# Background attention placed by a small planner into FFN steps, with a second accumulator bank, grouped k features and loads in halves

## The chip, the cores and the metric

The kernel runs on one core of one Trainium2 chip. The metric is the time of one execution in microseconds (us), the lower the better. The kernel before has a slow state, in which the granted TensorE clock is lower and the run about 5 us longer (fast runs 266.2 to 267.3 us, those with a recorded clock at 0.951 to 0.964; slow runs 270 to 274 at 0.927 to 0.950). Only fast runs are used for times. The trace of the kernel before that is read below fell in the slow state (271.9 us, span 269.8), so some 5 us of what it shows are that state's and not the kernel's.

PE is TensorE's matmul, PEld its weight load, DVE is VectorE, ACT is ScalarE, POOL is GpSimd, SP is SyncE.

## The reference

```python
# q, k, v: (4 batches, 4 heads, 1088, 32); S1, S2: (8, 32); w_in (128, 2048), w_out (2048, 128); all float32
phi(x) = outer(S1 x, S2 x)                     # 64 features for each token and head
kv = phi(k)^T v ;  z = sum(phi(k))             # over the 1088 tokens
attn = (phi(q) kv) / (phi(q) z + 1e-6)
x = attn, heads side by side: (4352, 128)
out = max(x @ w_in, 0)^2 @ w_out
```

For each batch the attention must be finished chunk by chunk (three chunks of 384, 384 and 320 tokens) before the FFN of that chunk can start. So the kernel computes the attention of batch n in the background of the FFN of batch n - 1.

## The kernel before

One FFN step handles one of 16 slices of 128 hidden units for one chunk: `pg` (float16 matmul into PSUM), relu on ACT into `gt`, square on DVE or ACT into `g2`, `po` (float32, two matmul instructions, x2 in the timelines) accumulated over 16 steps. There are 4 x 3 x 16 = 192 steps; `pg` and relu run three steps ahead of `po` (LA = 3). In the traces an instruction of PE or DVE that has to wait also holds up what stands behind it on its engine (below, an `nd` matmul of PE waits 1.65 us, and the FFN's matmuls with it).

The names in code and traces: `kT` is k transposed, `kf` its two feature factors (S1 k and S2 k), `fs` their copy by ACT (the matmuls here all write into tiles of the PSUM pools `psf` and `psa`, called banks below), `kp` their product phi(k), and `kv` the matmuls that sum phi(k)^T v in PSUM. `qT`, `qc`, `qb`, `qa` and `qp` are the same for q. `nd` holds numerator and denominator of attn. The x chain divides them in ten DVE operations, from `den` to `xs` and `beta` (`xs` is scaled for float16; `beta` undoes that at the output). `xp` transposes `xs` on PE, and its copy `xT` is the input of the FFN. `oT`, `op` and `ob` bring the FFN's result to the output.

```python
    # pools: pg 3 banks, po 2, and one bank each for acc, feat, tr
    psf = ctx.enter_context(tc.tile_pool(name="psf", bufs=3, space=bass.MemoryType.PSUM))
    psa = ctx.enter_context(tc.tile_pool(name="psa", bufs=1, space=bass.MemoryType.PSUM))
...
    def a_kp(b, g):
        kf = st[b, "kf", g]
        fs = wpool.tile([128, 3 * 96], F32, tag="fs", name="fs")
        kp = wpool.tile([128, 3 * 256], F32, tag="kp", name="kp", bufs=3)
        segs = [(0, 3, 128)] if g < 2 else [(0, 2, 128), (2, 1, 64)]
        for i, n, w in segs:
            nc.scalar.copy(fs[0:w, 96 * i : 96 * i + 96 * n], kf[0:w, 96 * i : 96 * i + 96 * n])
        for i in range(3):
            w = TW[3 * g + i]
            nc.vector.tensor_tensor(
                out=_ap(kp, 0, w, 256 * i, [[32, 8], [8, 4], [1, 8]]),
                in0=_ap(fs, 0, w, 96 * i, [[4, 8], [1, 4], [0, 8]]),
                in1=_ap(fs, 0, w, 96 * i + 32, [[8, 8], [0, 4], [1, 8]]),
                op=mult,
            )
        st[b, "kp", g] = kp

    def a_kv(b, t):
        if t == 0:
            st[b, "kvp"] = psa.tile([128, 512], F32, tag="acc", name="kvp")
        kvp = st[b, "kvp"]
        kp = st[b, "kp", t // 3]
        w = TW[t]
        for e in range(E):
            nc.tensor.matmul(
                kvp[:, 132 * e : 132 * e + 132],
                kp[0:w, 256 * (t % 3) + 128 * e : 256 * (t % 3) + 128 * e + 128],
                va[b % 2][0:w, 132 * t : 132 * t + 132],
                start=(t == 0 and e == 0),
                stop=(t == NT - 1),
                skip_group_check=True,
            )
...
    def a_nd(b, t):
        ch, o = t // 3, t % 3
        if o == 0:
            st[b, "nd", ch] = psa.tile([128, 512], F32, tag="acc", name="nd")
        nd = st[b, "nd", ch]
        w = TW[t]
        for e in range(E):
            nc.tensor.matmul(
                nd[0:w, 132 * o : 132 * o + 132],
                st[b, "qp", ch, e][:, 128 * o : 128 * o + w],
                st[b, "kvz"][:, 132 * e : 132 * e + 132],
                start=(e == 0),
                stop=(e == E - 1),
            )

    def a_xs(b, ch):

        if ch == 0:
            st[b, "xT"] = bpool.tile([128, S], F16, tag="xT", name="xT")
            st[b, "beta"] = bpool.tile([128, NT], F32, tag="beta", name="beta")
        nd, beta = st[b, "nd", ch], st[b, "beta"]
        xs = wpool.tile([128, 3 * 128], F16, tag="xs", name="xs")
        for o, n, w in ([(0, 3, 128)] if ch < 2 else [(0, 2, 128), (2, 1, 64)]):
            ...  # ten dependent DVE ops: den, rden, mx, m1, mm, mp, rm, sc, xs, beta
...
    def ffn1(i):
        b, ch, c = steps[i]
        n = min(384, S - 384 * ch)
        pg = psf.tile([128, 512], F32, tag="pg", name="pg")
        nc.tensor.matmul(
            pg[:, 0:n],
            w_in[:, 128 * c : 128 * c + 128],
            st[b, "xT"][:, 384 * ch : 384 * ch + n],
        )
        gt = fpool.tile([128, 384], F32, tag="gt", bufs=3, name="gt")
        g2 = fpool.tile([128, 384], F32, tag="g2", name="g2")
        nc.scalar.activation(gt[:, 0:n], pg[:, 0:n], Relu)
        if c % 4 == 3:
            nc.scalar.activation(g2[:, 0:n], gt[:, 0:n], Square)
        else:
            nc.vector.tensor_tensor(out=g2[:, 0:n], in0=gt[:, 0:n], in1=gt[:, 0:n], op=mult)
        g2s[i] = g2

    def ffn2(i):
        b, ch, c = steps[i]
        n = min(384, S - 384 * ch)
        if c == 0:
            st["po", b, ch] = psf.tile([128, 512], F32, tag="po", bufs=2, name="po")
        nc.tensor.matmul(
            st["po", b, ch][:, 0:n],
            w_o[:, 128 * c : 128 * c + 128],
            g2s.pop(i)[:, 0:n],
            start=(c == 0),
            stop=(c == NFF - 1),
        )
...
            # background of batch n, placed by hand in the 48 FFN steps of batch n - 1
            at(4, a_v, n)
            for part in range(3):
                at(5 + part, a_kT, n, part)
            for g in range(3):
                at(8 + 3 * g, a_kf, n, g, psa, "feat")
                at(9 + 3 * g, a_kp, n, g)
            for t in range(NT):
                at(18 + t, a_kv, n, t)
            at(17, a_qT, n, 0)
            at(18, a_qT, n, 1)
            for ch in range(3):
                at(19 + 4 * ch, a_qc, n, ch, psa, "feat")
                at(20 + 4 * ch, a_qb, n, ch)
                at(21 + 4 * ch, a_qa, n, ch, 0)
                at(22 + 4 * ch, a_qa, n, ch, 1)
            at(27, a_kvz, n)
            for ch in range(3):
                for i in range(3):
                    at(29 + 5 * ch + i, a_nd, n, 3 * ch + i)
                at(32 + 5 * ch, a_xs, n, ch)
                at(35 + 5 * ch, a_xp, n, ch)
```

Of the kernel before, what the change touches and what calls it, by code (L numbers as in the profile page):

```python
# [20 lines left out]

@with_exitstack
def kernel(
# [16 lines left out]

    G = S // 32
    DFF = 2048
    NFF = DFF // 128
    NT = (S + 127) // 128
    TW = [min(128, S - 128 * t) for t in range(NT)]
    CHUNKS = [(0, 3), (3, 6), (6, 9)]
    E = 2
    LA = 3

# [12 lines left out]
    psf = ctx.enter_context(tc.tile_pool(name="psf", bufs=3, space=bass.MemoryType.PSUM))  # L62
# [4 lines left out]
    s_nat = cpool.tile([128, 32], F32)  # L67
    nc.gpsimd.memset(s_nat[:], 0.0)
    for h in range(H):
        nc.sync.dma_start(s_nat[32 * h : 32 * h + 8, :], S1[:, :])  # L70
        nc.scalar.dma_start(s_nat[32 * h + 8 : 32 * h + 16, :], S2[:, :])

    def load_qk(dst, src, b, c0, c1, eng):
        eng.dma_start(
            dst[:, c0:c1],
            bass.AP(src.tensor, src.offset + b * H * S * D + c0, [[G * D, 128], [1, c1 - c0]]),
        )

    def load_v(vn, b, eng):

        base = v.offset + b * H * S * D
        for p0 in range(4):
            eng.dma_start(
                _ap(vn, 32 * p0, 32, 0, [[256, H], [1, 256]]),
                bass.AP(v.tensor, base + 8 * p0 * D, [[G * D, 32], [S * D, H], [1, 8 * D]]),
            )
        for p0 in range(2):
            eng.dma_start(
                _ap(vn, 32 * p0, 32, 1024, [[32, H], [1, 32]]),
                bass.AP(v.tensor, base + (32 + p0) * D, [[G * D, 32], [S * D, H], [1, D]]),  # L90
            )
# [7 lines left out]

    alloc_loads(0)  # L100
    load_qk(kn[0], k, 0, 0, 512, nc.sync)
    load_qk(kn[0], k, 0, 512, S, nc.scalar)
    load_v(vn[0], 0, nc.sync)
    load_qk(qn[0], q, 0, 0, 512, nc.scalar)
    load_qk(qn[0], q, 0, 512, S, nc.scalar)

# [3 lines left out]
    for c in range(2):  # L110
        nc.sync.dma_start(
            w_in32[:, 1024 * c : 1024 * c + 1024], moe_w_in[:, 1024 * c : 1024 * c + 1024]
        )
    for c in range(2):
        nc.sync.dma_start(
            _ap(w_o, 0, 128, 1024 * c, [[128, 8], [1, 128]]),
            bass.AP(
                moe_w_out.tensor,
                moe_w_out.offset + c * 1024 * 128,
                [[128, 128], [128 * 128, 8], [1, 128]],  # L120
            ),
        )
# [5 lines left out]
    nc.gpsimd.memset(sq[:], 0.0)  # L128
    iden = cpool.tile([128, 128], F32)
# [3 lines left out]
    hmask = cpool.tile([128, E * 132], F32)  # L133
    nc.gpsimd.memset(hmask[:], 0.0)
    for h in range(H):
        nc.gpsimd.memset(_ap(hmask, 32 * h, 32, 33 * h, [[132, E], [1, 33]]), 1.0)
    va = []
    for i in range(2):
        t_ = cpool.tile([128, NT * 132], F32, tag=f"va{i}", name=f"va{i}")
        nc.gpsimd.memset(_ap(t_, 0, 128, 32, [[33, NT * H]]), 1.0)  # L140
        va.append(t_)
# [22 lines left out]
    def a_v(b):  # L164
        a = va[b % 2]
        nc.gpsimd.tensor_copy(  # L166
            _ap(a, 0, 128, 0, [[33, H], [132, 8], [1, 32]]),
            _ap(vn[b], 0, 128, 0, [[256, H], [32, 8], [1, 32]]),
        )
        nc.gpsimd.tensor_copy(  # L170
            _ap(a, 0, 64, 8 * 132, [[33, H], [1, 32]]),
            _ap(vn[b], 0, 64, 1024, [[32, H], [1, 32]]),
        )

    def a_kT(b, part):
        if part == 0:
            st[b, "kT"] = bpool.tile([128, S], F32, tag="kT", bufs=1, name="kT")
        kT = st[b, "kT"]
        if part < 2:
            nc.vector.transpose(  # L180
                _ap(kT, 0, 128, 64 * part, [[32, 2], [128, 8], [1, 32]]),
                _ap(kn[b], 0, 128, 512 * part, [[256, 2], [32, 8], [1, 32]]),
# [4 lines left out]
    def a_qT(b, part):  # L187
        if part == 0:
            st[b, "qT"] = bpool.tile([128, S], F32, tag="qT", bufs=1, name="qT")
        c0, c1 = ((0, 512), (512, S))[part]  # L190
        nc.vector.transpose(st[b, "qT"][:, c0:c1], qn[b][:, c0:c1])  # L191

    def a_kf(b, g, pool, tag):
        kT = st[b, "kT"]
        kf = pool.tile([128, 512], F32, tag=tag, name="kf")
        for i in range(3):
            w = TW[3 * g + i]
            nc.tensor.matmul(  # L198
                kf[0:w, 96 * i : 96 * i + 96],
                kT[:, 128 * (3 * g + i) : 128 * (3 * g + i) + w],  # L200
                sk[:, :],
            )
        st[b, "kf", g] = kf

    def a_kp(b, g):
        kf = st[b, "kf", g]
        fs = wpool.tile([128, 3 * 96], F32, tag="fs", name="fs")
        kp = wpool.tile([128, 3 * 256], F32, tag="kp", name="kp", bufs=3)
        segs = [(0, 3, 128)] if g < 2 else [(0, 2, 128), (2, 1, 64)]
        for i, n, w in segs:  # L210
            nc.scalar.copy(fs[0:w, 96 * i : 96 * i + 96 * n], kf[0:w, 96 * i : 96 * i + 96 * n])  # L211
        for i in range(3):
            w = TW[3 * g + i]
            nc.vector.tensor_tensor(  # L214
                out=_ap(kp, 0, w, 256 * i, [[32, 8], [8, 4], [1, 8]]),
                in0=_ap(fs, 0, w, 96 * i, [[4, 8], [1, 4], [0, 8]]),
                in1=_ap(fs, 0, w, 96 * i + 32, [[8, 8], [0, 4], [1, 8]]),
                op=mult,
            )
        st[b, "kp", g] = kp  # L220

    def a_kv(b, t):
        if t == 0:
            st[b, "kvp"] = psa.tile([128, 512], F32, tag="acc", name="kvp")
        kvp = st[b, "kvp"]
        kp = st[b, "kp", t // 3]
        w = TW[t]
        for e in range(E):
            nc.tensor.matmul(  # L229
                kvp[:, 132 * e : 132 * e + 132],  # L230
                kp[0:w, 256 * (t % 3) + 128 * e : 256 * (t % 3) + 128 * e + 128],
                va[b % 2][0:w, 132 * t : 132 * t + 132],
# [12 lines left out]
    def a_qc(b, ch, pool, tag):  # L245
        c0 = 384 * ch
        n = min(384, S - c0)
        qc = pool.tile([128, 512], F32, tag=tag, name="qc")
        nc.tensor.matmul(qc[:, 0:n], sq[:, :], st[b, "qT"][:, c0 : c0 + n])  # L249
        st[b, "qc", ch] = qc  # L250

    def a_qb(b, ch):
        n = min(384, S - 384 * ch)
        qb = wpool.tile([128, 384], F32, tag="qb", name="qb")
        nc.vector.stream_shuffle(in_=st[b, "qc", ch][:, 0:n], out=qb[:, 0:n], mask=mask_b)
        st[b, "qb", ch] = qb

    def a_qa(b, ch, e):
        n = min(384, S - 384 * ch)
        qa = wpool.tile([128, 384], F32, tag="qa", name="qa")  # L260
        qp = bpool.tile([128, 384], F32, tag="qp", bufs=4, name="qp")
        nc.vector.stream_shuffle(in_=st[b, "qc", ch][:, 0:n], out=qa[:, 0:n], mask=mask_a[e])  # L262
        nc.vector.tensor_tensor(  # L263
            out=qp[:, 0:n], in0=qa[:, 0:n], in1=st[b, "qb", ch][:, 0:n], op=mult
# [3 lines left out]
    def a_nd(b, t):  # L268
        ch, o = t // 3, t % 3
        if o == 0:  # L270
            st[b, "nd", ch] = psa.tile([128, 512], F32, tag="acc", name="nd")
        nd = st[b, "nd", ch]
        w = TW[t]
        for e in range(E):
            nc.tensor.matmul(  # L275
                nd[0:w, 132 * o : 132 * o + 132],
                st[b, "qp", ch, e][:, 128 * o : 128 * o + w],
# [5 lines left out]
    def a_xs(b, ch):  # L283

        if ch == 0:
            st[b, "xT"] = bpool.tile([128, S], F16, tag="xT", name="xT")
            st[b, "beta"] = bpool.tile([128, NT], F32, tag="beta", name="beta")
        nd, beta = st[b, "nd", ch], st[b, "beta"]
        xs = wpool.tile([128, 3 * 128], F16, tag="xs", name="xs")
        for o, n, w in ([(0, 3, 128)] if ch < 2 else [(0, 2, 128), (2, 1, 64)]):  # L290
            def small(tag, m=4):
                return wpool.tile([128, 12], F32, tag=tag, name=tag)[0:w, 0 : m * n]
            den, rden, mx, m1, sc = (small(x) for x in ("den", "rden", "mx", "m1", "sc"))
            mm, mp, rm = (small(x, 1) for x in ("mm", "mp", "rm"))
            nc.vector.tensor_scalar(
                out=den, in0=_ap(nd, 0, w, 132 * o + 32, [[33, 4 * n]]),
                scalar1=1e-6, scalar2=None, op0=add,
            )
            nc.vector.reciprocal(rden, den)  # L299
            nc.vector.tensor_reduce(  # L300
                out=mx, in_=_ap(nd, 0, w, 132 * o, [[33, 4 * n], [1, 32]]),
                axis=AX, op=amax, apply_absolute_value=True,
            )
            nc.vector.tensor_tensor(out=m1, in0=mx, in1=rden, op=mult)
            nc.vector.tensor_reduce(
                out=mm, in_=_ap(m1, 0, w, 0, [[4, n], [1, 4]]),
                axis=AX, op=amax, apply_absolute_value=True,
            )
            nc.vector.tensor_scalar(  # L309
                out=mp, in0=mm, scalar1=1.0 / 1024.0, scalar2=1.0 / 1024.0, op0=mult, op1=add,  # L310
            )
            nc.vector.reciprocal(rm, mp)
            nc.vector.tensor_tensor(
                out=_ap(sc, 0, w, 0, [[4, n], [1, 4]]),
                in0=_ap(rden, 0, w, 0, [[4, n], [1, 4]]),
                in1=_ap(rm, 0, w, 0, [[1, n], [0, 4]]),
                op=mult,
            )
            nc.vector.tensor_tensor(  # L319
# [226 lines left out]
```

## Time and profile before

| | before |
|---|---|
| time, fast runs of the first measurement | 266.75 us median (266.44 to 267.25) |
| profiled run | 271.9 us, span 269.8, state slow |
| first `pg` matmul | 27.4 us |
| FFN part, first `pg` to last `po` | 27.4 to 263.2 us |

From the page of the kernel before: busy time of the engines and, in 40 equal slices of the span, the busy tenths of PE and the granted clock of TensorE.

```profile
PE 227.8 (84%) x1032; PEld 148.8 (55%) x1032; DVE 162.2 (60%) x469; ACT 137.0 (51%) x319; POOL 8.9 (3%) x29
...
PE   0884996959997779999997697999997779999991
...
PEclk9999597999997997999997979999999997999998
```

PE is the busiest engine, but three times its row sinks to 7 and 6, in the third chunk of each of the first three batches (it also sinks to 6 and 5 in the first batch, between 40 and 61 us). The view of stretches, cut at the ends of FFN chunks, has for each stretch its length, the busy time of each engine with the number of instructions, and the granted clock:

```profile
core 0: us, PE busy (x) PEld busy (x) DVE busy (x) ACT busy (x) POOL busy (x), PEclk, DMA share, GB/s
...
27.40:54.40 27.00, 24.14 (x100) 15.47 (x100) 18.67 (x57) 12.12 (x27) 0.00 (x0) 0.84 0.00 1
54.40:78.20 23.80, 21.03 (x106) 14.28 (x105) 16.88 (x50) 11.56 (x27) 0.00 (x0) 1.00 0.03 9
...
139.80:166.20 26.40, 20.06 (x90) 12.88 (x89) 15.92 (x58) 11.18 (x27) 1.28 (x2) 0.87 0.29 72
...
181.80:202.10 20.30, 20.30 (x104) 14.18 (x103) 14.55 (x37) 10.93 (x27) 0.00 (x0) 1.00 0.04 10
...
239.30:252.50 13.20, 13.20 (x53) 7.52 (x53) 6.57 (x13) 10.38 (x25) 0.00 (x0) 1.00 0.06 16
```

The stretch 181.8 to 202.1 is full: PE has no gap, so with its clock at 1.00 only less PE work could shorten it. The stretch 139.8 to 166.2 has 6.3 us without PE work, and its clock is 0.87. No stretch has DVE or ACT busy for its whole length (the largest share is 79%, ACT from 239.3 to 252.5): no other engine is full. The view of waits, for PE alone (who waited, for whom, us in total, how often, longest):

```profile
PE nd L275 <- DVE beta L325: 9.1, 5, 2.5
PE kf L198 <- DVE kT L185: 7.9, 1, 7.9
PE xp L336 <- DVE xs L319: 6.0, 6, 1.5
...
PE kf L198 <- DVE kT L180: 2.7, 1, 2.7
```

The second line is the start of the kernel; the others are stalls inside the FFN part. One of them in the timeline (start, duration, engine, line, operation; in brackets the idle time before and what ended it):

```profile
80.70 0.16 DVE L295 TENSOR_SCALAR den<-nd 128x12 f32<-128x12 f32 x1
...
82.60 0.56 DVE L319 TENSOR_TENSOR xs<-nd,sc 128x384 f16<-128x384 f32 x1
83.07 0.15 DVE L325 TENSOR_TENSOR beta<-mp 128x3 f32<-128x3 f32 x1
...
83.30 0.69 PE L275 MATMUL nd<-kvz,qp 128*128 128x132 f32 x4 [1.65 <-DVE beta L325]
...
83.96 1.27 PE L371 MATMUL po<-g_729,w_o 128*128 128x320 f32 x2
...
88.11 0.70 PE L371 MATMUL po<-g_776,w_o 128*128 128x320 f32 x2
```

The x chain runs for 2.5 us from `den` to `beta`. PE reaches the next chunk's `nd`, which needs the same accumulator bank, 1.65 us too early and stands still, with all FFN work behind it. Then the pair of `po` matmuls takes 1.27 us; in the same view an undisturbed pair takes 0.70. This stall is paid twice, once as idle time and once as a slow clock: the packed trace's clock records, which the views show only as means, have half clock for 3.41 us from 83.95.

### The profile page before, as it was taken

How to read it: one execution, taken by the hardware profiler on the slowest of the kernel's cores; microseconds unless marked ns; L12 is line 12 of the kernel's file. 1: busy time of each engine (PE TensorE's matmuls, PEld its weight loads, DVE VectorE, ACT ScalarE, POOL GpSimd, SP SyncE). 2: the span in 40 equal slices, each digit the busy share in tenths (PEclk: the TensorE clock that was granted, in tenths of full speed). 3: DMA queues.
4: the chain of work that ended last, by engine and by line, in shares of the span. 5: the costliest groups of instructions: out<-in, count | busy, mean ns of one | idle time of the engine just before them, and what ended most of it. 6: DMA issues, size and time to landing. Idle time of an engine off the chain costs nothing.

```text
span 269.8 us, 3312 instructions
## 1 busy us (share of the span) xinstructions
PE 227.8 (84%) x1032; PEld 148.8 (55%) x1032; DVE 162.2 (60%) x469; ACT 137.0 (51%) x319; POOL 8.9 (3%) x29
## 2 busy tenths in 40 slices
PE   0884996959997779999997697999997779999991
PEld 0682464737665545567665464567764535555660
DVE  2654774686765673767766636576768563545440
ACT  1220552464363446765463355767445446787861
POOL 4201000000000200000000100000000000000000
PEclk9999597999997997999997979999999997999998
DMA  5992000000006400001004600001001000001000
GB/s 141 276 324 68 0 2 0 0 7 26 0 0 166 115 0 4 20 1 32 0 0 139 139 2 0 26 1 32 0 0 29 2 1 0 24 1 29 7 24 24
DMA packets 11897, 11.23 MB, mean 42 GB/s; under 512 B 1896, under 2 KB 10344, under 8 KB 11880
## 3 DMA queue, kind: packets, MB, share of 16 engines
q1 hardware_dynamic: 11384, 10.17, 14.0%
q10 hardware_dynamic: 496, 0.86, 1.2%
q8 instruction: 8, 0.13, 0.2%
q14 instruction: 9, 0.07, 0.1%
HBM read 8.79 MB, written 2.23 MB: 41 GB/s over the span
## 4 chain that ended last, share of the span: by engine, by line
PE 72%; DVE 19%; ACT 3%; issue 2%; DMA 2%; ACTq 1%; POOL 0%; DVEq 0%; POOLq 0%
PE po L371 38%; PE pg L352 10%; PE nd L275 7%; PE kvp L229 7%; PE kf L198 4%; PE qc L249 3%; DVE xs L319 3%; DVE mx L300 2%; DMA kn<-in_k_dram 2%; ACT gt L359 2%; DVE qp L263 1%; DVE mp L309 1%; DVE rden L299 1%; PE op L391 1%; PE xp L336 1%
## 5 line engine op out<-in xcount | busy, mean ns | idle before, releaser
L359 ACT ACTIVATE gt<-pg 128x384 f32<-128x384 f32 (+1 forms) x192 | 89.2, 471 | 85.6 <-PE pg L352 79.9
L352 PE MATMUL pg<-xT,w_in 128*128 128x384 f16 (+1 forms) x192 | 63.5, 333 | 0.6 <-ACT xT L342 0.6
L275 PE MATMUL nd<-kvz,qp 128*128 128x132 f32 (+1 forms) x144 | 25.1, 302 | 11.9 <-DVE beta L325 9.1
L275 PEld LDWEIGHTS nd<-kvz,qp 128*128 128x128 f32 (+1 forms) x144 | 21.5, 198 | 21.9 <-issue 16.3
L352 PEld LDWEIGHTS <-w_in 128*128 128x128 f16 x192 | 19.8, 103 | 16.3 <-issue 3.4
L198 PE MATMUL kf<-sk,kT 128*128 128x96 f32 (+1 forms) x72 | 12.6, 324 | 10.6 <-DVE kT L185 7.9
L214 DVE TENSOR_TENSOR kp<-fs 128x256 f32<-128x256 f32 (+1 forms) x36 | 13.9, 443 | 8.6 <-ACT fs L211 8.6
L198 PEld LDWEIGHTS kf<-sk,kT 128*128 128x128 f32 (+1 forms) x72 | 11.3, 227 | 14.1 <-issue 8.0
L342 ACT COPY xT<-xp 128x384 f16<-128x384 f16 (+1 forms) x12 | 5.5, 456 | 22.3 <-PE xp L336 22.3
L263 DVE TENSOR_TENSOR qp<-qa,qb 128x384 f32<-128x384 f32 (+1 forms) x24 | 12.9, 537 | 6.3 <-PE nd L275 5.3
L229 PEld LDWEIGHTS kvp<-va_124,kp 128*128 128x128 f32 (+1 forms) x72 | 10.7, 190 | 5.3 <-issue 1.1
L262 DVE STREAM_SHUFFLE qa<-qc 128x384 f32<-128x384 f32 (+1 forms) x24 | 13.5, 562 | 0.0
L249 PE MATMUL qc<-qT,sq 128*128 128x384 f32 (+1 forms) x24 | 10.6, 526 | 3.3 <-DVE qT L191 3.3
L397 ACT ACTIVATE ob<-op,beta 128x128 f32<-128x128 f32 (+1 forms) x36 | 10.5, 363 | 4.6 <-PE op L391 4.5
L229 PEld LDWEIGHTS kvp<-va_122,kp 128*128 128x128 f32 (+1 forms) x72 | 10.7, 211 | 3.5 <-POOL va_122 L166 0.7
L229 PE MATMUL kvp<-va_124,kp 128*128 128x132 f32 (+1 forms) x72 | 11.2, 279 | 0.0
L336 PE MATMUL xp<-iden_114,xs 128*128 128x128 f16 (+1 forms) x36 | 5.3, 249 | 7.0 <-DVE xs L319 6.0
L229 PE MATMUL kvp<-va_122,kp 128*128 128x132 f32 (+1 forms) x72 | 11.1, 299 | 0.0
L336 PEld LDWEIGHTS <-xs 128*128 128x128 f16 (+1 forms) x36 | 3.5, 113 | 12.8 <-DVE xs L319 8.1
L211 ACT COPY fs<-kf 128x288 f32<-128x288 f32 (+2 forms) x16 | 4.9, 335 | 6.3 <-PE kf L198 6.3
L319 DVE TENSOR_TENSOR xs<-nd,sc 128x384 f16<-128x384 f32 (+2 forms) x16 | 7.3, 455 | 0.5
L382 ACT COPY oT<-po 128x384 f32<-128x384 f32 (+1 forms) x12 | 5.5, 460 | 3.2 <-PE po L371 2.2
(649 smaller groups left out, 407.2 us busy)
## 6 DMA issues: line engine op xcount, KB each, us to landing
vn<-in_v_dram SPq DMA_DIRECT2D x16, 128.0 KB
out_dram<-ob SPq DMA_DIRECT2D x32, 64.0 KB
kn<-in_k_dram SPq DMA_DIRECT2D x3, 544.0 KB
qn<-in_q_dram SPq DMA_DIRECT2D x3, 544.0 KB
w_in_98<-in_moe_w_in_dram SPq DMA_DIRECT2D x2, 512.0 KB
w_o<-in_moe_w_out_dram SPq DMA_DIRECT2D x2, 512.0 KB
kn<-in_k_dram ACTq DMA_DIRECT2D x1, 288.0 KB
qn<-in_q_dram ACTq DMA_DIRECT2D x1, 288.0 KB
```

What stands on the lines that cost most here:

```text
L198: nc.tensor.matmul(kf[0:w, 96 * i : 96 * i + 96], kT[:, 128 * (3 * g + i) : 128 * (3 * g + i) + w], sk[:, :],)
L214: nc.vector.tensor_tensor(out=_ap(kp, 0, w, 256 * i, [[32, 8], [8, 4], [1, 8]]), in0=_ap(fs, 0, w, 96 * i, [[4, 8], [1, 4], [0, 8]]), in1= ...
L229: nc.tensor.matmul(kvp[:, 132 * e : 132 * e + 132], kp[0:w, 256 * (t % 3) + 128 * e : 256 * (t % 3) + 128 * e + 128], va[b % 2][0:w, 132 * ...
L249: nc.tensor.matmul(qc[:, 0:n], sq[:, :], st[b, "qT"][:, c0 : c0 + n])
L262: nc.vector.stream_shuffle(in_=st[b, "qc", ch][:, 0:n], out=qa[:, 0:n], mask=mask_a[e])
L263: nc.vector.tensor_tensor(out=qp[:, 0:n], in0=qa[:, 0:n], in1=st[b, "qb", ch][:, 0:n], op=mult)
L275: nc.tensor.matmul(nd[0:w, 132 * o : 132 * o + 132], st[b, "qp", ch, e][:, 128 * o : 128 * o + w], st[b, "kvz"][:, 132 * e : 132 * e + 132 ...
L319: nc.vector.tensor_tensor(out=_ap(xs, 0, w, 128 * o, [[32, 4 * n], [1, 32]]), in0=_ap(nd, 0, w, 132 * o, [[33, 4 * n], [1, 32]]), in1=_ap( ...
L336: nc.tensor.transpose(xp[:, 128 * i : 128 * i + w], xs[0:w, 128 * i : 128 * i + 128], iden16[0:w, 0:w],)
L352: nc.tensor.matmul(pg[:, 0:n], w_in[:, 128 * c : 128 * c + 128], st[b, "xT"][:, 384 * ch : 384 * ch + n],)
L359: nc.scalar.activation(gt[:, 0:n], pg[:, 0:n], Relu)
L371: nc.tensor.matmul(st["po", b, ch][:, 0:n], w_o[:, 128 * c : 128 * c + 128], g2s.pop(i)[:, 0:n], start=(c == 0), stop=(c == NFF - 1),)
```

## The change

The intent is to keep PE from ever standing before an input that is not there yet. A small planner puts every background task into an FFN step by its needs: on PE at least two steps after what it depends on, on DVE and ACT one, and not into a step whose engine is full. It also sends a square to ACT when ACT's planned load with relu and square would stay below DVE's with the square. Around it: a second `acc` bank (paid for with the third `pg` bank), k features in one product for four tiles, the x chain in three pieces on whole (zero-padded) tiles, and a reordered start that takes k and v in halves of whole tiles. The diff, cut to its core:

```diff
+class _Plan:
+
+
+
+    LAG = {"PE": 2, "DVE": 1, "ACT": 1, "POOL": 1, "SP": 1}
+
+    def __init__(self, nsteps, cap):
+        self.n, self.cap = nsteps, cap
+        self.load = {e: [0.0] * nsteps for e in cap}
+        self.at, self.slots = {}, [[] for _ in range(nsteps)]
+        self.late = []
+
+    def fix(self, key, eng, dur, step, f, *args):
+        self.at[key] = step
+        self.load[eng][step] += dur
+        self.slots[step].append((f, args))
+
+    def add(self, key, eng, dur, needs, f, *args, not_in=(), first=0, lag=None):
+        s = first
+        for k in needs:
+            s = max(s, self.at[k] + (self.LAG[eng] if lag is None else lag))
+        while s < self.n - 1 and (
+            (self.load[eng][s] > 0 and self.load[eng][s] + dur > self.cap[eng])
+            or s % 16 in not_in
+        ):
+            s += 1
+        self.fix(key, eng, dur, s, f, *args)
+        return s
... (the loads of the first batch: S1 and S2 all from ACT; k, v and q from SP, v in pieces of 64 KB)
-    s_nat = cpool.tile([128, 32], F32)
-    nc.gpsimd.memset(s_nat[:], 0.0)
-    for h in range(H):
-        nc.sync.dma_start(s_nat[32 * h : 32 * h + 8, :], S1[:, :])
-        nc.scalar.dma_start(s_nat[32 * h + 8 : 32 * h + 16, :], S2[:, :])
+    s_nat = cpool.tile([128, 32], F32)
+    nc.vector.memset(s_nat[:], 0.0)
+    for s_, r0 in ((S1, 0), (S2, 8)):
+        for h in range(H):
+            nc.scalar.dma_start(s_nat[32 * h + r0 : 32 * h + r0 + 8, :], s_[:, :])
...
-    psf = ctx.enter_context(tc.tile_pool(name="psf", bufs=3, space=bass.MemoryType.PSUM))
+    psf = ctx.enter_context(tc.tile_pool(name="psf", bufs=2, space=bass.MemoryType.PSUM))
... (k features: groups of 4, 4 and 1 whole tiles, one product per group)
+    def a_fs(b, g):
+
+        n = KG[g][1]
+        kf = st[b, "kf", g]
+        fs = wpool.tile([128, 4 * 96], F32, tag="fs", name="fs")
+        nc.scalar.copy(fs[:, 0 : 32 * n], _ap(kf, 0, 128, 0, [[96, n], [1, 32]]))
+        nc.scalar.copy(fs[:, 128 : 128 + 64 * n], _ap(kf, 0, 128, 32, [[96, n], [1, 64]]))
+        st[b, "fs", g] = fs
... (in a_kp)
+        fs = st[b, "fs", g]
+        kp = wpool.tile([128, 4 * 256], F32, tag="kp", name="kp", bufs=3)
+        nc.vector.tensor_tensor(
+            out=_ap(kp, 0, 128, 0, [[32, 8 * n], [8, 4], [1, 8]]),
+            in0=_ap(fs, 0, 128, 0, [[4, 8 * n], [1, 4], [0, 8]]),
+            in1=_ap(fs, 0, 128, 128, [[8, 8 * n], [0, 4], [1, 8]]),
+            op=mult,
+        )
...
+            st[b, "kvp"] = psa.tile([128, 512], F32, tag="acc", bufs=2, name="kvp")
... (the x chain, a_xs before, becomes a_x1, a_x2, a_x3 on whole tiles; xp and xT, op and ob become separate tasks)
-        if c % 4 == 3:
+        if sq_on_act:
... (the planner's table)
+    P = _Plan(NS + 4, {"PE": 0.95, "DVE": 1.2, "ACT": 0.6, "POOL": 9.0, "SP": 9.0})
+    for m in range(B * 3):
+        b, ch = divmod(m, 3)
+        s0 = 16 * (m + 1)
+        P.fix(("oT", b, ch), "ACT", 0.46, s0 - 1, f_oT, b, ch)
+        P.fix(("op", b, ch), "PE", 0.5, s0 + 1, f_op, b, ch)
+        P.fix(("ob", b, ch), "ACT", 0.5, s0 + 2, f_ob, b, ch)
+        P.load["ACT"][min(s0 + 3, NS + 3)] += 0.5
...
+    def nd_tasks(b, chs):
+        for ch in chs:
+            need = [("qp", b, ch, 1)]
+            need += [("kvz", b)] if ("kvz", b) in P.at else []
+            need += [("x3", b, ch - 2)] if ("x3", b, ch - 2) in P.at else []
+            for t in range(3 * ch, 3 * ch + 3):
+                P.add(("nd", b, t), "PE", 0.45, need, a_nd, b, t)
+            P.add(("x1", b, ch), "DVE", 0.9, [("nd", b, 3 * ch + 2)], a_x1, b, ch)
+            P.add(("x2", b, ch), "DVE", 0.9, [("x1", b, ch)], a_x2, b, ch)
+            P.add(("x3", b, ch), "DVE", 0.7, [("x2", b, ch)], a_x3, b, ch)
+            P.add(("xp", b, ch), "PE", 0.4, [("x3", b, ch)], a_xp, b, ch, not_in=tr_busy)
+            at = P.add(("xT", b, ch), "ACT", 0.46, [("xp", b, ch)], a_xT, b, ch)
+            assert at < 48 * b + 16 * ch - LA, (b, ch, at)
+
...
+    def act_square(i):
+
+        s = max(i - LA, 0)
+        return P.load["ACT"][s] + 0.47 + 0.41 < P.load["DVE"][s] + 0.46
 
     for i in range(LA):
-        ffn1(i)
-    for i, (b, ch, c) in enumerate(steps):
-        if ch == 0 and c == 0:
-            slots = background(b)
-        if i + LA < len(steps):
-            ffn1(i + LA)
-        ffn2(i)
-        if c == NFF - 1:
-            ffn_evac(b, ch)
... (the new loop: ffn1 with act_square, ffn2, then the tasks that the planner put into the step)
```

## The prediction

> **What bounds it now.** TensorE (PE). The page gives PE 84% busy, DVE 60%, ACT 51%; the chain of waits is PE 72%, DVE 19%. Undisturbed, one FFN step (pg, then two po matmuls) takes 0.81 us at 384 columns, 0.67 at 320 (timeline, last batch): 146 us for 192 steps. Background PE work in the FFN part, from the timeline: 0.45 us per token tile for kv and for nd, 0.215 per tile for kf, 0.65 per qc, about 0.33 per group of xp or op transposes: 47 us. So the FFN part needs 193 us of PE. It takes 236 (27.4 to 263.2). The other 42 us are stalls and slow clock. The view of stretches: 139.8 to 166.2 has PE busy 20.1 of 26.4 us at clock 0.87; 181.8 to 202.1 is 100% busy at clock 1.00. The waits of PE name the reason: nd waits for the x chain (beta 9.1 us, xs 1.6; one acc bank), xp for xs 6.0, kf for kT 2.7. While PE waits, relu and squares starve too.
> [...] after an idle of 1.65 us at 81.7 a po pair took 1.27 us, not 0.54. Stalls cost twice.
>
> **What changes.**
> - Second acc bank (paid with pg 3 to 2): the beta/xs waits before nd should nearly go.
> - Planner: dependents come 2 steps later on PE, 1 on DVE/ACT; the ten-op x chain (2.5 us straight) is split in three. Squares go to ACT where DVE is loaded (about 75 of 192, was 48).
> - Grouped kp: three 256-wide ops take 1.10 us; one 1024-wide should take about 1.15, saving about 0.3 per four tiles. The x chain runs once in the last chunk, not twice (about 1.4 us of DVE per batch). Padding adds some tenths per batch.
> - Startup: kf begins after half of k; v copied on ACT; second qT and qc before the x chain. First pg now 27.4; I expect about 24.3.
>
> Tallying trace durations along the new program order: PE 193, DVE 137, ACT 145 us. If every step cost its busiest engine, 211; if slack of three steps evens it out, 197.
>
> **Sum of the profiled span:** startup 24.3 + first-step latency 1.6 + PE 193 + residual stalls 9 + tail 6.5 = 234.4; timed runs lie about 2 us above the span: **236 us, range 229 to 246**. Nearly all of the gain (31 us) is on the critical path: about 27 from stalls and clock in the FFN part, 3 from startup. Faster by over 2%: 0.96; same 0.03; slower 0.01.
>
> **What would show it.** Right: waits of nd for beta/xs under 2 us, of xp for xs under 2 us; PE busy share above 92% with PE busy time falling (fewer slow matmuls); mean clock 0.97 or more; first pg between 23 and 26 us; batches 1 and 2 near 54 us (were 63 and 58.5), batch 0 near 60 (was 76); kp at 1.1 to 1.25 us. Wrong on the banks: PE waits at pg for gt (relu) over 5 us in total.
>
> **What would make it wrong.** (1) Steps with relu and square (0.96 us of ACT against 0.81 of PE) with two pg banks make ACT the pacer: nearer 245. (2) Batch 0 is crowded (PE 18.3, DVE 15.8, ACT 15.9 in its first 16 steps) and may stall 5 us. (3) v arrives in 512-byte pieces, twice as many packets; the startup gain may vanish. (4) The slow clock persists although PE is dense.

Startup 24.3, latency 1.6, PE 193, residual stalls 9 and tail 6.5 came to 234.4, and to 236 us for a timed run. "Stalls cost twice" holds for six of eleven long stalls. The 1.15 us for a 1024-wide product was the author's estimate; 1.22 was measured. That relu and squares starve shows after the 1.65 us stall at 81.7: ACT is idle for 2.42 us before the next relu (84.20), for want of `pg`, and DVE for 3.61 us before a square (88.78), for want of relu. The packets of v did double: the packed trace before has 2048 packets of 1024 bytes and 6400 of 512, the one after none of 1024 and 10496 of 512.

## The result, and the profile after

The changed kernel takes 231.62 us (median of 4 fast runs, 231.07 to 232.51). The ratio is 0.868, with a 95% interval of 0.865 to 0.872. Ratios here are the mean time of one kernel's fast runs over that of the other's of the same rounds, so not quite the ratio of the medians quoted. A second measurement gave 231.52.

The same lines of the page, now of the changed kernel, with a span of 229.6 us:

```profile
PE 208.6 (91%) x1032; PEld 144.4 (63%) x1032; DVE 142.7 (62%) x375; ACT 149.2 (65%) x358; POOL 9.0 (4%) x33
...
PE   0497499989999999999999999999999999999990
...
PEclk9999889999999999999999999999999999999996
```

The count of matmuls is the same (x1032), yet PE is busy for 19 us less. The view of stretches, with its cuts at the corresponding chunk ends:

```profile
26.96:48.00 21.04, 20.62 (x98) 13.80 (x98) 14.81 (x43) 16.75 (x37) 0.00 (x0) 0.92 0.01 2
48.00:67.30 19.30, 18.49 (x95) 12.89 (x94) 9.96 (x21) 11.78 (x31) 0.00 (x0) 1.00 0.04 11
...
120.80:135.30 14.50, 14.50 (x86) 10.66 (x85) 12.02 (x39) 12.68 (x32) 2.31 (x3) 1.00 0.46 131
...
198.90:212.00 13.10, 13.10 (x53) 7.42 (x52) 8.70 (x17) 8.67 (x20) 0.00 (x0) 1.00 0.06 17
```

The worst stretch before (139.8 to 166.2, third chunk of the second batch) took 26.4 us; its counterpart (120.8 to 135.3) takes 14.5 and is full. The second chunk of the last batch, which has no background, hardly changed (13.2 and 13.1). The clock column is no witness for the start: it counts time before a trace's first clock record (here at 17.09 us) as full, so it shows 1.00 for 0 to 26.96 us, in which the eighteen `kf` took 4.13 us (2.22 in a_best below). The waits of PE:

```profile
PE kf L240 <- DVE kT L226: 9.1, 1, 9.1
PE xp L386 <- DVE xs L370: 1.9, 1, 1.9
PE nd L316 <- DVE qp L305: 1.7, 2, 1.1
...
PE pg L406 <- ACT gt L413: 0.4, 1, 0.4
```

The first three all lie before the first `pg` (26.96 us). In the FFN part PE waits under 3 us in 196.

Where the time went, by adding up the stretches of the two traces:

| | before (slow-state trace) | after |
|---|---|---|
| first `pg` | 27.4 | 27.0 |
| FFN part | 235.8 | 195.7 |
| of it PE busy | 212.9 | 194.3 |
| of it PE without work | 22.9 | 1.5 |
| tail after the last `po` | 6.6 | 6.9 |

So 40 us of the FFN part went: 21 of idle time, and 19 because nearly the same matmuls ran faster. By the clock records 25.8 us of the FFN part lay at half clock before and 3.4 after; half of the difference, an estimate of 11 us, is the clock's part of the 19, and the rest was not worked out. Up to 5 us of this is the slow state of the trace before; the timed difference of fast runs is 35 us.

The start did not change by much. Its marks in the timeline, before and then after:

```profile
3.85 0.21 DVE L144 STREAM_TRANSPOSE s_T<-s_nat 128x32 f32<-128x32 f32 x1 [3.85 <-DMA s_nat<-in_S_dram]
...
7.90 4.21 PE L198 MATMUL kf<-sk,kT 128*128 128x96 f32 x18 [7.90 <-DVE kT L185]
```

```profile
0.94 4.07 ACTq L138 DMA_DIRECT2D s_nat<-in_S_dram  x8
1.66 5.56 SPq L111 DMA_DIRECT2D vn<-in_v_dram  x8
...
6.84 0.21 DVE L190 STREAM_TRANSPOSE s_T<-s_nat 128x32 f32<-128x32 f32 x1 [5.93 <-DMA s_nat<-in_S_dram]
...
9.05 4.13 PE L240 MATMUL kf<-sk,kT 128*128 128x96 f32 x18 [9.05 <-DVE kT L226]
```

With all eight loads of S1 and S2 on one queue, their issue alone takes 4.07 us, `s_T` starts 3 us later, and the first `kf` 1.15 us later than before (DVE makes `s_T` and `sk` before `kT`, so both inputs of `kf` come late). The start gains 1.6 us between `kf` and the first `pg`, and keeps 0.4.

The product of the k features, before in pieces of 256 and then of 1024 elements (minimum, median and maximum duration in ns):

```profile
L214 DVE TENSOR_TENSOR kp<-fs x36: 384/418/1272, 9.9 to 183.2; 128x256 f32<-128x256 f32 x32, 64x256 f32<-64x256 f32 x4
```

```profile
L258 DVE TENSOR_TENSOR kp<-fs x12: 418/1220/1226, 11.7 to 154.8; 128x1024 f32<-128x1024 f32 x8, 128x256 f32<-128x256 f32 x4
```

So four times the elements took 1220 ns in one product, 2.9 times the 418 of a piece. In the trace before three pieces in a row took 1.10 us (at 9.94 us); four at that pace would be 1.47, so the grouping saves about 0.25 us per four tiles, an estimate from these figures (0.3 was expected).

### The profile page after: what moved, and what is told of

The parts are those of the page before. It is cut to its first block, busy times and chain, and to the rows that moved or that the text cites. A ratio compares the mean times of both kernels' runs of the same rounds, so it can differ in the third digit from the quotient of the medians.

```text
span 229.6 us, 3199 instructions
## 1 busy us (share of the span) xinstructions
PE 208.6 (91%) x1032; PEld 144.4 (63%) x1032; DVE 142.7 (62%) x375; ACT 149.2 (65%) x358; POOL 9.0 (4%) x33
## 4 chain that ended last, share of the span: by engine, by line
PE 88%; ACT 4%; DMA 2%; DVE 2%; SPq 1%; issue 1%; ACTq 0%; DVEq 0%
PE po L425 50%; PE pg L406 13%; PE kvp L272 8%; PE nd L316 7%; PE kf L240 4%; PE qc L290 3%; DMA vn<-in_v_dram 2%; PE op L444 2%; ACT gt L413 1%; PE xp L386 1%; SPq L111 1%; ACT xT L395 1%; DVE qp L305 0%; SPq L101 0%; ACT oT L436 0%
## 5 line engine op out<-in xcount | busy, mean ns | idle before, releaser
L316 PEld LDWEIGHTS nd<-kvz,qp 128*128 128x128 f32 x144 | 19.7, 190 | 6.2 <-DVE qp L305 2.1
L316 PE MATMUL nd<-kvz,qp 128*128 128x132 f32 x144 | 20.4, 278 | 1.7 <-DVE qp L305 1.7
L240 PE MATMUL kf<-sk,kT 128*128 128x96 f32 x72 | 11.4, 309 | 9.1 <-DVE kT L226 9.1
L240 PEld LDWEIGHTS kf<-sk,kT 128*128 128x128 f32 x72 | 11.4, 226 | 11.4 <-issue 9.0
L272 PEld LDWEIGHTS kvp<-va_120,kp 128*128 128x128 f32 x72 | 10.7, 190 | 4.2
L300 DVE STREAM_SHUFFLE qa<-qc 128x384 f32<-128x384 f32 x24 | 13.1, 591 | 0.0
L272 PEld LDWEIGHTS kvp<-va_117,kp 128*128 128x128 f32 x72 | 11.4, 222 | 2.5 <-issue 0.2
L258 DVE TENSOR_TENSOR kp<-fs 128x1024 f32<-128x1024 f32 (+1 forms) x12 | 11.4, 954 | 2.4 <-ACT fs L251 2.4
L305 DVE TENSOR_TENSOR qp<-qa,qb 128x384 f32<-128x384 f32 x24 | 12.2, 548 | 0.0
L272 PE MATMUL kvp<-va_117,kp 128*128 128x132 f32 x72 | 11.8, 312 | 0.0
L272 PE MATMUL kvp<-va_120,kp 128*128 128x132 f32 x72 | 11.1, 277 | 0.0
L290 PE MATMUL qc<-qT,sq 128*128 128x384 f32 x24 | 9.9, 495 | 0.0
```

What stands on the lines that cost most here:

```text
L240: nc.tensor.matmul(kf[:, 96 * i : 96 * i + 96], kT[:, 128 * (t0 + i) : 128 * (t0 + i) + 128], sk[:, :])
L258: nc.vector.tensor_tensor(out=_ap(kp, 0, 128, 0, [[32, 8 * n], [8, 4], [1, 8]]), in0=_ap(fs, 0, 128, 0, [[4, 8 * n], [1, 4], [0, 8]]), in1 ...
L272: nc.tensor.matmul(kvp[:, 132 * e : 132 * e + 132], kp[:, 256 * (t % 4) + 128 * e : 256 * (t % 4) + 128 * e + 128], va[b % 2][:, 132 * t : ...
L290: nc.tensor.matmul(qc[:, 0:384], sq[:, :], qT[:, 384 * ch : 384 * ch + 384])
L300: nc.vector.stream_shuffle(in_=st[b, "qc", ch][:, 0:384], out=qa[:, :], mask=mask_a[e])
L305: nc.vector.tensor_tensor(out=qp[:, :], in0=st[b, "qa", ch, e][:, :], in1=st[b, "qb", ch][:, :], op=mult)
```

## The experiments

Twelve kernels ran, in three groups of four, each group beside the kernel before. All gave correct results. Each group ran on another chip, and the kernel before was mostly slow there (one fast run near 266 us in the first group, three in the second, none in the third). So differences within a group are the safest; for the second group the record's own verdict against the kernel before is "unclear", at ratios of 0.865 to 0.923. The question is which part of a change of many parts carries the 35 us. Two theories stood at first: PLACEMENT (dependents stood too close behind the DVE work that feeds them) and BANK (the single `acc` bank).

**b_acc2: the banks alone, in the kernel before.**

```diff
-tile_pool(name="psf", bufs=3
+tile_pool(name="psf", bufs=2
-psa.tile([128, 512], F32, tag="acc", name="kvp")      # and the same for nd
+psa.tile([128, 512], F32, tag="acc", bufs=2, name="kvp")
```

> The kernel before with only the banks changed (acc 2, pg 2). Theory BANK (the single acc bank is what stalls PE): the wait of nd for beta and xs (10.7 us) goes, squares are no longer starved behind it, the time falls to about 245 us. Theory PLACEMENT (dependents stand too close behind the DVE chain that feeds them): the same wait goes, but xp still waits for xs (6 us before) and po for squares queued behind the 2.5 us x chain; about 255 to 262 us.

Measured: 259.09 us (258.41 to 260.63), 7 us less than the fast runs before. The waits of `nd` are gone, but `xp` now waits 9.9 us, more than the 6.0 before:

```profile
PE xp L336 <- DVE xs L319: 5.1, 8, 1.2
PE xp L336 <- DVE beta L325: 4.8, 4, 1.5
```

Of 16.7 us of waits at these two, 9.9 are left, one instruction further on. This is what PLACEMENT expected; BANK's 245 was missed by 14.

**b_space: other step numbers by hand, one bank, nothing else.**

```diff
-            for ch in range(3):
-                at(19 + 4 * ch, a_qc, n, ch, psa, "feat")     # qb, qa, qa in the 3 steps after
+            for ch, s in enumerate((19, 23, 31)):
+                at(s, a_qc, n, ch, psa, "feat")
...
-                    at(29 + 5 * ch + i, a_nd, n, 3 * ch + i)
-                at(32 + 5 * ch, a_xs, n, ch)
-                at(35 + 5 * ch, a_xp, n, ch)
+                    at(29 + 6 * ch + i, a_nd, n, 3 * ch + i)
+                at(32 + 6 * ch, a_xs, n, ch)
+                at(36 + 6 * ch if ch < 2 else 47, a_xp, n, ch)
```

> The kernel before, one acc bank, with only the step numbers of background work moved by hand for batches 1 to 3: nd every 6 steps instead of 5, x chain 3 steps before the next nd, xp 3 or 4 steps after the x chain, the third chunk's qc/qb/qa 4 steps later. PLACEMENT: nd waits under 3 us, batches 1 and 2 near 55 us each, total 245 to 252 us (batch 0 untouched). BANK: the one bank still stalls nd, 258 us or more.

Measured: 250.47 us (247.79 to 251.37), 16 us less than before: nearly half of the whole gain from a few integers. The `nd` waits fell from 10.7 to 3.0 us, those of `xp` for the x chain from 6.0 to 3.1, and batches 1 and 2 took 54.0 and 53.8 us, all as PLACEMENT expected (its "under 3" just missed). The first `kf` wait (2.7 us) stayed.

**a_acc1: the changed kernel with one bank.** `pg` goes back to three banks, and the planner is told that `nd` and `kv` need the x chain that last used the bank.

```diff
-            need += [("x3", b, ch - 2)] if ("x3", b, ch - 2) in P.at else []
+            need += [("x3", b, ch - 1)] if ("x3", b, ch - 1) in P.at else []
-            ... [("kp", n, t // 4), ("v", n, t // 4)], a_kv, n, t)
+            ... [("kp", n, t // 4), ("v", n, t // 4), ("x3", n - 1, 2)], a_kv, n, t)
```

> The changed kernel with one acc bank (pg back to 3), the planner told that nd needs the previous chunk's x chain done. PLACEMENT: the planner finds room; within 2% of the changed kernel (at most 236 us). BANK: over 240 us, with PE waits of nd for x3.

Measured: 231.18 us (229.76 to 232.87), the same as the changed kernel (231.62). BANK falls: with the planner, a second `acc` bank in place of a third `pg` bank is worth nothing here.

**a_lag1: the planner's distances cut by one step.**

```diff
-    LAG = {"PE": 2, "DVE": 1, "ACT": 1, "POOL": 1, "SP": 1}
+    LAG = {"PE": 1, "DVE": 0, "ACT": 0, "POOL": 0, "SP": 0}
```

> The changed kernel, two banks, but the planner's distance cut from 2 steps to 1 on PE and from 1 to 0 on the other engines. PLACEMENT: PE waits come back (nd for qp, xp for xs, kv for kp), 240 us or more. BANK: two banks and the load caps are enough; within 2% of 231.6 us.

Measured: 240.76 us (239.99 to 240.92), 9 us slower than the changed kernel. In the FFN part PE waits for the DVE again: `xp` for xs 3.1 us, `qc` for qa 2.0, `kf` for kT 0.5 and `nd` for qp 0.2; 1.5 us more are waits for ACT. PLACEMENT is right.

The second group asks whether the spacing alone does it (ORDER) or needs the relief of DVE (PARTS). The changed kernel ran beside it as the measure.

> The changed kernel unaltered, as the measure for the three beside it on the same chip. Every theory: 231.6 us, within 1%.

Measured: 231.52 us (231.07 to 232.7).

**a_plain: planner and start kept, most other parts undone.** (Whole tiles, the x chain once instead of twice in the last chunk, and the separate `xT`, `op` and `ob` tasks stay.) One bank as in a_acc1, every fourth square on ACT, k features in 256-wide products, the x chain in one piece:

```diff
-            P.add(("x1", b, ch), "DVE", 0.9, [("nd", b, 3 * ch + 2)], a_x1, b, ch)
-            P.add(("x2", b, ch), "DVE", 0.9, [("x1", b, ch)], a_x2, b, ch)
-            P.add(("x3", b, ch), "DVE", 0.7, [("x2", b, ch)], a_x3, b, ch)
+            P.add(("x3", b, ch), "DVE", 2.5, [("nd", b, 3 * ch + 2)], a_x, b, ch)
...
-            ffn1(i + LA, act_square(i + LA))
+            ffn1(i + LA, (i + LA) % 4 == 3)
```

> The changed kernel's planner and startup, with every other part undone: one acc bank, three pg banks, squares fixed (every fourth on ACT), k features in 256-wide ops, the ten-op x chain in one piece of 2.5 us (the planner told so). ORDER theory (the planner's spacing alone carries the gain): at most 236 us. PARTS theory (spacing needs the relief of DVE and the split chain): 240 us or more, with PE waits of xp or po behind the undivided chain.

Measured: 247.33 us (246.13 to 247.56). ORDER's 236 is missed by 11, as PARTS expected: in the FFN part `xp` waits 11.9 us for xs.

```profile
PE xp L392 <- DVE xs L371: 11.9, 10, 1.7
```

**a_sq4: the fixed squares alone** (the last two lines of that diff, and the same rule for the first three steps).

> The changed kernel with the squares fixed, every fourth on ACT, instead of by load. ORDER: within 1% of 231.6 us. PARTS: DVE backs up where background work lies; 235 us or more, with PE waits of po for g.

Measured: 234.54 us (233.06 to 235.13), 3.0 us over the changed kernel: between the two expectations.

**a_xwhole: the undivided x chain alone** (the first four lines).

> The changed kernel with the x chain in one piece (planned as 2.5 us of DVE in one step) instead of three steps. ORDER: within 1% of 231.6 us, since xp still comes two steps later. PARTS: squares queue 2.5 us behind the chain and po waits for g; 236 us or more.

Measured: 233.32 us (232.50 to 233.72), 1.8 us over: within ORDER's 1%, and PARTS' 236 is missed.

One bank cost 0, the squares 3.0, the chain 1.8; all together cost 15.8. Either the parts interact, or the k features cost 11. The third group tells.

**a_sqx: fixed squares and undivided chain, nothing else.**

> The changed kernel with both the fixed squares and the undivided x chain (each alone cost 3.0 and 1.8 us; all parts undone together cost 16). If these two interact (a 2.5 us chain plus its share of squares does not fit in the two steps before xp): 241 us or more, PE waits of xp for xs over 6 us. If costs add: about 236 us, and the rest of the 16 us belongs to one bank or ungrouped k features.

Measured: 245.01 us (244.68 to 247.86), 13.5 us over the changed kernel of the second group. Added singly the two give 4.8. They interact, and they are nearly all of what a_plain lost. One such place in the timeline of a_sqx:

```profile
136.16 0.49 DVE L422 TENSOR_TENSOR g<-gt 128x320 f32<-128x320 f32 x1 [1.08 <-ACT gt L418]
136.57 0.16 DVE L330 TENSOR_SCALAR den<-nd 128x12 f32<-128x12 f32 x1
...
138.94 0.15 DVE L376 TENSOR_TENSOR beta<-mp 128x3 f32<-128x3 f32 x1
139.01 0.89 DVE L422 TENSOR_TENSOR g<-gt 128x320 f32<-128x320 f32 x2
...
139.08 0.42 PE L391 MATMUL xp<-iden,xs 128*128 128x128 f16 x3 [1.54 <-DVE xs L370]
```

The chain holds DVE from 136.57 to 139.09 and two squares queue behind it. Two FFN steps of a 320-column chunk last about 1.35 us (0.67 each), so `xp`, planned two steps later, is there too early. The length of the chain alone does not explain this, for a_xwhole has the same chain and the same plan for its background tasks. The corresponding place there:

```profile
127.52 0.17 DVE L330 TENSOR_SCALAR den<-nd 128x12 f32<-128x12 f32 x1 [0.25 <-PE nd L316]
...
130.03 0.42 PE L391 MATMUL xp<-iden,xs 128*128 128x128 f16 x3 [0.53 <-DVE xs L370]
```

The chain takes about 2.5 us in both. But in a_xwhole it starts 0.04 us after its last `nd` matmul (in 11 of 12 chains), in a_sqx 1.05 to 1.61 us after it (again in 11 of 12): the square at 136.16 stands before it on DVE. The planner had sent only 11 more squares to ACT (59 against 48), but other ones; which go seems to matter more than how many. None of this loss shows as clock: in a_sqx `xp` waits 10.4 us in the FFN part, and the clock records show no half clock there after 31.8 us (mean clock of its profiled run 0.979, of the changed kernel's 0.983).

**p_lag4: is that only a matter of distance?** a_plain with `xp` planned four steps after the chain.

```diff
-            P.add(("xp", b, ch), ..., a_xp, b, ch, not_in=tr_busy)
+            P.add(("xp", b, ch), ..., a_xp, b, ch, not_in=tr_busy, lag=4)
```

> The version with every part but the planner undone (247.3 us), with one number changed: xp four steps after the x chain instead of two. If distance is what counts: the xp waits (11.9 us) fall under 2 us and the time to 234 to 238 us. If DVE is overloaded on the whole: the waits move to nd or po and the time stays over 243 us.

Measured: 245.09 us (244.72 to 245.88), 2 us better than a_plain and no more. Its PE waits:

```profile
PE nd L317 <- DVE qp L306: 5.7, 6, 1.6
PE nd L317 <- DVE beta L377: 4.8, 3, 1.8
PE po L431 <- DVE g L423: 2.8, 4, 1.1
PE xp L392 <- DVE xs L371: 1.6, 1, 1.6
```

This view covers the start too: the whole `xp` wait (1.6 us) and 1.7 us of the first line lie before the first `pg`. In the FFN part the `xp` wait fell from 11.9 us to nothing, and about 11 us of waits appeared at other dependents. So a longer distance for `xp` alone doesn't help: DVE is behind in these steps (10 of the 12 x chains start 1.05 to 1.4 us after their `nd`), and whoever comes next waits for it. A longer distance for every dependent was not tried.

**a_ssplit: the loads of S1 and S2 from two queues.**

```diff
-    for s_, r0 in ((S1, 0), (S2, 8)):
-        for h in range(H):
-            nc.scalar.dma_start(s_nat[32 * h + r0 : 32 * h + r0 + 8, :], s_[:, :])
+    for h in range(H):
+        nc.scalar.dma_start(s_nat[32 * h : 32 * h + 8, :], S1[:, :])
...   # after both loads of k
+    for h in range(H):
+        nc.sync.dma_start(s_nat[32 * h + 8 : 32 * h + 16, :], S2[:, :])
```

> The changed kernel with the eight loads of S1 and S2 issued from two queues (S1 from ACT, S2 from SP after k) instead of all from ACT. If sk, waiting for the last of the eight loads, is what ate the startup gain: s_T before 5 us (was 6.84), first kf near 6.8 us (was 9.05), first pg near 25 us (was 26.96), total about 229.7 us. If v (issued at 0.7 us a piece from one queue) is the bound: first pg within 0.5 us of 26.96.

Measured: 230.28 us (229.45 to 230.49). `s_T` starts at 5.74 us instead of 6.84, `kf` at 7.93 instead of 9.05, the first `pg` at 25.43 instead of 26.96. So these loads were part of what held up the start; splitting them won less than hoped at each mark. The 1.1 us won at `s_T` came with eight loads of 1 KB, whose issue from ACT alone had taken 4.07 us (0.51 each). Eight of v's loads of 64 KB took 5.56 us to issue from SP (0.70 each).

**a_best: that split, v of the first batch from two queues, and dummy matmuls in PE's idle time.**

```diff
+    wt = cpool.tile([128, 384], F16)
+    nc.vector.memset(wt[:], 1.0)
+    def warm(n):
+        wp = psa.tile([128, 512], F32, tag="tr", name="wp")
+        for _ in range(n):
+            nc.tensor.matmul(wp[:, 0:384], wt[:, 0:128], wt[:, :])
...
+    warm(20)          # ahead of the first kf
+    warm(8)           # ahead of the first batch's first xp
```

> The changed kernel with S1/S2 split as in a_ssplit, the first batch's v issued from two queues, and idle PE time at the start filled with dummy matmuls on a constant tile that nobody reads (20 before kf, 8 during the first x chain), so that its clock is up when kf and kv come. If the slow clock at the start is due to idling: kf 18 matmuls in about 2.2 us (was 4.1), kv likewise, first po pair 0.65 us (was 1.59), first pg near 21 to 22.5 us, total about 226 us. If not: no more than a_ssplit gives.

Measured: 227.45 us (226.67 to 228.29), the fastest of all, 2.8 us below a_ssplit beside it and 4.1 us below the changed kernel (231.57, the mean of its two medians, as it did not run in this group). First `pg` at 23.23 us, where 21 to 22.5 was expected. From its timeline:

```profile
1.37 5.01 PE L145 MATMUL wp<-wt 128*128 128x384 f16 x20 [1.37 <-DVE wt L140]
...
8.20 2.22 PE L249 MATMUL kf<-sk,kT 128*128 128x96 f32 x18 [1.82 <-DVE kT L235]
...
24.73 1.31 PE L434 MATMUL po<-g,w_o 128*128 128x384 f32 x2
```

The eighteen `kf` matmuls take 2.22 us, half of the 4.13 before the dummies. They are the same instructions on the same data, now after PE has been working; in a_ssplit, without the dummies, they took 4.12 us. The first sixteen `kvp` matmuls take 2.04 us instead of 3.86. The first `po` pair still takes 1.31 us (1.59 before; 0.81 in the steady state), though the eight dummies in the x chain ran until 21.71 us. That part of the expectation was missed, and the total is 1.5 us above the 226 hoped for. How the gain divides between the dummies and v from two queues was not measured apart.

The dummies show the change of pace themselves: up to about 4.5 us, 3.2 us after the first, they are issued 0.32 us apart, then 0.16. The first clock record of this trace, of full clock, is at 4.63 us, just where they double their pace; so the difference in the `kf` is put down to the clock.

## Why the prediction was right

The measured 231.62 us lies inside the range of 229 to 246, 4.4 us below the predicted 236. Term by term, in the trace of the changed kernel:

| term of the sum | predicted | measured |
|---|---|---|
| first `pg` | 24.3 | 26.96 |
| first-step latency (first `pg` to first `po`) | 1.6 | 1.56 (28.52 - 26.96) |
| PE work and residual stalls | 193 + 9 = 202 | 194.2 (28.52 to 222.7) |
| tail | 6.5 | 6.9 |
| timed run over span | 2 | 1.8 |

- **The PE floor was right.** The tally of 193 us from undisturbed durations in the trace before is what the FFN part now costs, to about 1 us.
- **"Residual stalls 9" was mis-sized**: about 1 instead of 9. I had feared ACT as the new pacer with two `pg` banks; PE waits 0.4 us for relu in all. The experiments show why the stalls are this few: dividing the chain and moving squares together keep DVE from falling behind. Either one undone costs 2 to 3 us, both 13.5: with fixed squares most x chains start 1 us or more late (in a_sq4 too, where the three pieces give a chain two more steps before `xp`), and undivided they have no time to spare.
- **"Startup 24.3" was mis-sized the other way.** I took the start of `kf` from k's arrival and missed that `sk` waits for the last of eight loads now on one queue. a_ssplit and a_best show that the gain was there to have (25.43 and 23.23). The two errors (7.8 too much, 2.7 too little) have opposite signs, so it is in part luck that the total is better than its terms.
- **The step "Second acc bank ... the beta/xs waits before nd should nearly go" was right as an observation and wrong as a cause.** The waits went, but a_acc1 shows that they go without the second bank (231.18), and b_acc2 that with the bank alone 9.9 us of waits stand at `xp` (259.09).
- **Checks:** mean clock 0.983 (0.97 or more: right). PE busy share 91% (above 92%: just missed, as the start did not shrink). Batches 1 and 2, from chunk end to chunk end: 51.0 and 50.3 us, where near 54 was expected; batch 0 57.3, where near 60 was. Squares on ACT: 76 of 192 (about 75: right). k features 1.22 us (1.1 to 1.25: right).
- **A slip in the text:** it sets a `po` pair of "1.27 us" against "0.54". The first is the timeline's duration, the second the chain's, which counts only what is not overlapped. In the timeline's terms it is 1.27 against 0.70, in the chain's 1.07 against 0.54. And its "Stalls cost twice" holds for six of the eleven long stalls of that trace, not for all.

How the 35 us arose: PE has a floor that was 193 us before as well. What stood between was order. Spacing alone, by hand, in part of the kernel gave 16 us (b_space). The planner with undivided chain and fixed squares gave about 19 (a_plain, 247.33; whole tiles are in it). The remaining 16 came from spreading the DVE work, and those two measures count only together. The bank gave nothing in the end. Grouping the k features was not tried alone; a_plain, with it and the second bank undone as well, was 2.3 us slower than a_sqx in another group, which bounds what both together do there.

Still open: how much of the start's gain in a_best is the clock; how little of the planner's spacing would be enough once DVE is relieved (a_lag1 tried one step less, at 9 us); and one run of the kernel before at 260.44 us, the only one below 266. It was not traced, but its mean clock of 0.983 is that kernel's highest (0.964 or less in its other runs with a recorded clock) and equals that of the changed kernel's trace. So some 6 of the 35 us may be clock that the kernel before loses in most runs but not in all: against that run the gain is 29 us.

## What to carry to other kernels

Where instructions of an engine wait in order, as here, an instruction put one step too early costs all that stand behind it (in a_lag1 one step less cost 9 us), so first add up the busiest engine's work from undisturbed durations: if the trace is far above that floor (here 236 us against 193) and no other engine is full, suspect the order first; a second buffer may only move the wait to the next dependent (here it won 7 of 35 us alone, and nothing beside the planner). Long DVE chains should be cut into pieces between which the pipeline's own short work can pass (1.8 us here), and work that can go to either of two engines should be sent where background load is not (3.0 us); undo such measures in pairs before calling one of them useless (13.5 us for both). Count the clock in: a stall of PE can also slow the matmuls after it (six of eleven long ones before the change, none of the ten `xp` waits of a_sqx; which of them do, these runs do not let one predict), and idle PE time at the start can be filled with dummy matmuls (in a_best 20 of them took the eighteen `kf` from 4.13 to 2.22 us).
